# A new hand-written order for a sketched-attention and feed-forward kernel, with other queues for its first loads and all rows of x through DRAM

## The chip, the cores and the metric

The kernel runs on one core of a Trainium2 chip. The metric is the time of one execution on the device, in microseconds. The core has a matrix engine (TensorE, PE in the profile; PEld are its weight loads), VectorE (DVE), ScalarE (ACT), GpSimd (POOL), and SyncE (SP), which here only issues DMAs. ACT can issue DMAs as well. Each engine works through its own instructions in order and waits for the others by semaphores; DMAs issued on SP and on ACT are moved by the core's 16 DMA engines.

## What is computed

```
def phi(x):                                        # x: (b, h, s, 32); S1, S2: (8, 32)
    a = einsum('rd,bhsd->bhsr', S1, x)
    b = einsum('rd,bhsd->bhsr', S2, x)
    return einsum('bhsi,bhsj->bhsij', a, b).reshape(..., 64)
q_p, k_p = phi(q), phi(k)                          # 4 batches, 4 heads, 1088 tokens
kv  = einsum('bhsf,bhsd->bhfd', k_p, v)
z   = k_p summed over s
x   = einsum('bhsf,bhfd->bhsd', q_p, kv) / (einsum('bhsf,bhf->bhs', q_p, z) + 1e-6)
x   = x with the heads side by side                # (4, 1088, 128)
xn  = (x - mean) / sqrt(var + 1e-6) * g_ln         # over the 128 columns
out = x + relu(xn @ w_ch1) @ w_ch2                 # 128 -> 512 -> 128
```

S1, S2 and the two weight matrices arrive as float64 and are turned into float32 on the chip, from their bit fields (the `w_` steps: exponent, mantissa, low word). "Words 0" are S1 and S2, "words 1" w_ch1, "words 2" w_ch2.

## The kernel before

The whole program is one list of steps, `PROGRAM` (lines 910 to 1001). A loop at its end calls the functions named there in that order, and each puts its instructions on the engine that the step names (V VectorE, A ScalarE, G GpSimd, S SyncE) or that the function fixes. There is no planner at run time: the list is the order on every engine, and an engine that waits holds up everything behind it in its own part of the list. A capital A, B, C, D, M, N, O or K in other places names one of the eight PSUM banks.

For each batch b the steps are these. `ld` loads k and q with 128 partitions of 34 rows, `ld_v` and `ld_vr` load v; batch 0's v is loaded whole and turned over by TensorE (`v_flip`, `v_cp`). `turn_g`, `turn_h` and `turn_r` (L434, L457, L452) transpose k and q on VectorE in 32 by 32 blocks; `k_feat` (L506) and `q_feat` (L629) multiply by the sketches, `k_tok` and `q_tok` transpose the features back. `k_prod` forms the 64 products per key, `k_val` (L560) sums them against v, `k_vcp`, `k_spr` and `k_rcp` spread the result for the numerators. `k_sum`, `k_zs`, `k_sc` (L531, L539, L545) and `k_sccp` (L553) bring the denominator into q's weights `skq`, on which `q_feat` depends. `q_ac`, `q_den`, `q_rec`, `q_a2`, `q_prod` and `q_turn` (L677) make the normalised query products, and `num` (L735) multiplies them with kv: 32 matmuls of 32 by 32 tiles at 16 positions of the array, four banks for the four row groups. Batch 0 does the first part of this in its own way (`q_dir`, `q_prod0`, `q_flip`, `fold` for w_ch1 times g, `num0`). Three small masks, `c_m2`, `c_m32` and `c_m8`, are made on VectorE (two instructions each, L206 and L207).

The result comes out transposed (`num_cp`, `num_r`), in chunks c: two per batch of 512 tokens (0 to 7) and two of 128 for what is left over (8 and 9). Per chunk, `hid` (L843) makes one of four blocks j of the hidden layer, `relu` (L851, L853) empties it to `hT`, and `sec` (L859) makes one of four blocks t of the second product. `hT` has two buffers, used in turn in the order of chunks 0, 1, 2, 3, 8, 4, 5, 6, 7, 9. For the statistics and the residual the chunk is needed with tokens on the partitions. Chunks 1 to 7 take it through DRAM: `row_turn` (L797) transposes blocks, `row_wr` (L802) writes, four `row_rd` (L808) read back. Chunks 0, 8 and 9 take it by TensorE: `row_pe` (L787) and a copy, `row_cp`. `st_bn`, `st_ag` and `st_pow` (L816 to L829) give the scale, `fin` (L872) or `fin_a` with `fin_g` (L878, L888) the sum, `store` the output.

`fill` and `bump` (L250, L244) are matmuls on ones whose result nobody reads; they stand where TensorE would wait.

The lines that the change and the prediction touch, beside `PROGRAM`:

## Time and profile before

| | us |
|---|---|
| median of 3 runs | 102.90 (102.72 to 105.06) |
| the profiled execution, whole time | 102.81 |
| its span in the profile | 100.9 |
| TensorE busy in the span | 95.3 |
| VectorE busy | 74.0 |
| GpSimd busy | 58.4 |
| ScalarE busy | 41.3 |
| end of the last `sec` on TensorE, from the span's start | 97.40 |

The profile shows one execution. Times in the views count from the start of the span; the whole time is the span and what lies around it. A busy PE is not the same as a PE at its peak, since matmuls are pipelined. A line that begins with an engine and a line of the kernel (L859) is a group of instructions; "out<-in" are the tiles written and read, a releaser after "<-" is what ended an engine's wait.

DMA before: 81 issues on SyncE and 27 on ScalarE. The page moves 13.85 MB; the transfers between `xd` and x or `xh` are the rows through DRAM.

### The profile page before, as it was taken

The numbers are of one execution on the slowest core, as the hardware profiler recorded it, in microseconds if no ns is written. First come the engines' busy times: TensorE is split into PE (matmuls) and PEld (weight loads), VectorE is DVE, ScalarE is ACT, GpSimd is POOL, SyncE is SP. The second block draws the span as 40 slices with busy tenths as digits, with TensorE's granted clock in tenths as the row PEclk, the third lists the DMA queues.
The fourth block names the chain that finished last, engine by engine and source line by source line (L and its number), as shares of the span: only waits on it lengthen the run. The fifth ranks groups of instructions, "written<-read, shape, count | busy, mean of one in ns | idle before, by whom it ended". The sixth has DMA issues, their size and how long they took to land.

```text
span 100.9 us, 3433 instructions
## 1 busy us (share of the span) xinstructions
PE 95.3 (94%) x1355; PEld 68.7 (68%) x1355; DVE 74.0 (73%) x239; ACT 41.3 (41%) x119; POOL 58.4 (58%) x83
## 2 busy tenths in 40 slices
PE   5988999999999999999999999999999999999960
PEld 5765668656656779656588669854469758959950
DVE  2878989789999599699089549999559079661630
ACT  2863754979700720755513353029640030253000
POOL 7115998999588926912999189809920540057000
PEclk9999999999999999999999999999999999999999
DMA  2989999893008760030023220346146445054242
GB/s 76 272 293 389 353 370 275 272 218 88 3 6 301 212 164 3 6 130 0 6 107 106 47 59 0 109 153 187 55 107 204 143 122 148 1 115 132 77 119 64
DMA packets 12367, 13.85 MB, mean 137 GB/s; under 512 B 2880, under 2 KB 8768, under 8 KB 12352
## 3 DMA queue, kind: packets, MB, share of 16 engines
q1 hardware_dynamic: 9968, 11.67, 38.8%
q10 hardware_dynamic: 2384, 1.97, 6.7%
q8 instruction: 10, 0.16, 0.7%
q14 instruction: 5, 0.04, 0.2%
HBM read 9.57 MB, written 4.06 MB: 135 GB/s over the span
## 4 chain that ended last, share of the span: by engine, by line
PE 78%; DMA 5%; POOL 5%; DVE 2%; ACT 2%; SPq 2%; issue 1%; ACTq 0%; POOLq 0%
PE bankO L859 8%; PE bankM L859 8%; DMA w_raw<-in_moe_w_ch_dram 5%; PE bankN L843 5%; PE bankK L560 5%; PE bankC L843 4%; PE bankK L843 4%; PE bankK L859 4%; PE bankB L843 3%; PE bankA L843 3%; PE bankD L843 3%; PE bankM L250 3%; PE bankA L859 3%; PE bankN L859 3%; POOL ob L888 2%; PE bankA L735 2%
## 5 line engine op out<-in xcount | busy, mean ns | idle before, releaser
L82 POOL TENSOR_TENSOR kp<-kf 128x1024 f32<-128x1024 f32 (+4 forms) x9 | 15.9, 1779 | 0.1
L827 POOL TENSOR_SCALAR va<-mv 128x4 f32<-128x4 f32 (+1 forms) x10 | 2.3, 228 | 18.2 <-DVE mv L822 17.7
L82 POOL TENSOR_TENSOR qp<-a,fq 128x1280 f32<-128x1280 f32 (+1 forms) x5 | 11.1, 2219 | 0.2
L859 PEld LDWEIGHTS bankO<-w,hT 128*128 128x128 f32 x80 | 9.7, 192 | 1.9 <-issue 1.9
L829 POOL TENSOR_TENSOR rstd<-va,mhalf 128x4 f32<-128x4 f32 (+1 forms) x10 | 10.3, 1034 | 0.8
L859 PE MATMUL bankO<-w,hT 128*128 128x128 f32 x80 | 10.4, 277 | 0.0
L859 PEld LDWEIGHTS bankM<-w,hT 128*128 128x128 f32 x72 | 9.0, 192 | 1.9 <-issue 1.9
L677 DVE STREAM_TRANSPOSE qpT<-qp 128x1280 f32<-128x1280 f32 (+1 forms) x7 | 9.6, 1365 | 0.0
L250 PE MATMUL bankM<-ones 128*128 128x256 f32 (+1 forms) x28 | 8.3, 440 | 1.2 <-DVE top L180 1.2
L859 PE MATMUL bankM<-w,hT 128*128 128x128 f32 x72 | 9.3, 275 | 0.0
L816 DVE BATCH_NORM_STATS2 st<-x 128x6 f32<-128x128 f32 x32 | 6.7, 272 | 2.5 <-issue 2.5
L250 PEld LDWEIGHTS bankM<-ones 128*128 128x128 f32 x28 | 5.7, 241 | 2.5 <-DVE top L180 1.2
L851 ACT ACTIVATE hT<-bankC 128x512 f32<-128x512 f32 (+1 forms) x6 | 3.3, 551 | 8.3 <-PE bankB L859 4.7
L843 PE MATMUL bankC<-xT,w 128*128 128x512 f32 x12 | 6.1, 592 | 0.0
L843 PE MATMUL bankN<-xT,w 128*128 128x512 f32 (+1 forms) x14 | 6.1, 516 | 0.0
L851 ACT ACTIVATE hT<-bankN 128x256 f32<-128x256 f32 (+1 forms) x6 | 3.0, 498 | 7.2 <-PE bankN L843 7.2
L82 POOL TENSOR_TENSOR a<-fq,rden 128x160 f32<-128x160 f32 (+1 forms) x6 | 2.8, 463 | 5.2 <-DVE rden L659 4.8
L560 PEld LDWEIGHTS bankK<-kp,vn 128*32 128x32 f32 x288 | 4.2, 110 | 2.3 <-issue 1.1
L851 ACT ACTIVATE hT<-bankK 128x512 f32<-128x512 f32 (+1 forms) x6 | 3.1, 522 | 6.2 <-PE bankK L843 5.3
L457 DVE STREAM_TRANSPOSE qT<-qn 128x512 f32<-128x512 f32 x8 | 5.5, 687 | 0.0
L843 PE MATMUL bankK<-xT,w 128*128 128x512 f32 (+1 forms) x12 | 5.4, 530 | 0.0
L735 PE MATMUL bankD<-qpT,kvr 32*32 32x288 f32 (+1 forms) x64 | 5.2, 386 | 0.0
(235 smaller groups left out, 255.2 us busy)
## 6 DMA issues: line engine op xcount, KB each, us to landing
kn<-in_k_dram SPq DMA_DIRECT2D x3, 544.0 KB, 6.2
qn<-in_q_dram SPq DMA_DIRECT2D x3, 544.0 KB, 6.4
vn<-in_v_dram SPq DMA_DIRECT2D x12, 128.0 KB, 4.5
xd<-xh SPq DMA_DIRECT2D x5, 256.0 KB, 2.6
x<-xd SPq DMA_DIRECT2D x20, 64.0 KB, 2.0
out_dram<-ob SPq DMA_DIRECT2D x19, 64.0 KB, 1.7
out_dram<-ob ACTq DMA_DIRECT2D x13, 64.0 KB, 1.9
w_raw<-in_moe_w_ch_dram SPq DMA_DIRECT2D x2, 256.0 KB, 4.0
```

Of the source, the lines that this page charges most:

```text
L82: by[eng].tensor_tensor(out=o, in0=a, in1=b, op=ALU.mult)
L250: pe.matmul(M[0][:, 0:w], ones[:, 0:P], ones[:, 0:w], start=True, stop=True)
L457: dve.transpose(_ap(dst[b % 2], 0, P, P * 4 * half, [[32, 4], [P, 4], [1, 32]]), src[b][:, 512 * half : 512 * half + 512],)
L560: pe.matmul(KV[D * h : D * h + D, 0:F], vn[b][:, TW * h + D * u : TW * h + D * (u + 1)], kp[:, H * F * u + F * h : H * F * u + F * (h + 1) ...
L677: dve.transpose(_ap(qpT, 0, P, 32 * u0, [[32, u1 - u0], [TW, 8], [1, 32]]), qp[:, H * F * u0 : H * F * u1])
L735: pe.matmul(X[r][D * h : D * h + D, o : o + w], kvr[b % 2][rows, DM * f + D * h : DM * f + D * h + D], qpT[rows, c : c + w], start=(f == 0 ...
L816: dve.bn_stats(out=sts[slot(c)][:, 6 * t : 6 * t + 6], in_=row_ap(c, t))
L827: pool.tensor_scalar(out=vas[slot(c)][:, 0:n], in0=_ap(mvs[slot(c)], 0, P, 1, [[2, n]]), scalar1=1e-6, scalar2=None, op0=ALU.add)
L829: pool.tensor_tensor(out=rstds[slot(c)][:, 0:n], in0=vas[slot(c)][:, 0:n], in1=mhalf[:, 0:n], op=ALU.pow)
L843: pe.matmul(banks[z][:, 0:n], w1[:, P * j : P * (j + 1)], cols(c)[:, a : a + n], start=True, stop=True)
L851: act.activation(o, i, AF.Relu)
L859: pe.matmul(banks[z][:, DM * t : DM * (t + 1)], h[:, 512 * j + P * t : 512 * j + P * (t + 1)], w2[:, DM * j : DM * (j + 1)], start=(j == 0 ...
```

## The change

Three things change in the code. The loop in `num` has its two inner loops exchanged: the four matmuls that follow each other now have four row groups, not four column groups. The set `through_dram` holds all ten chunks. And `PROGRAM` is a new list: nearly every step stands elsewhere, several have another engine or bank. Of its 585 steps, `row_pe` and `row_cp` of chunks 0, 8 and 9 and `sk_0` are gone; for those chunks `row_turn`, `row_wr` and four `row_rd` each come in. The fills are the same in number and length.

Cut to what the text speaks of:

```diff
         for f in range(2):
-            for r in range(4):
-                for h in range(H):
+            for h in range(H):
+                for r in range(4):
                     rows, o = slice(32 * r, 32 * r + 32), 32 * u0
...
-    through_dram = set((1, 2, 3, 4, 5, 6, 7, ))
+    through_dram = set((0, 1, 2, 3, 4, 5, 6, 7, 8, 9))
...
-    ld_w S 1 2 4; c_ones; ld_g A; c_small; c_ac 0; ld_s A 0; ld_s S 1; c_vpad 0; c_kvb; c_vpad 1;
-    fill 1 128; ld S k 0 0 16; c_act; c_pads 1; c_pads 0; fill 4 256; c_iota; ld S k 0 16 34;
-    c_ac 1; c_m2; c_ident; ld_w S 1 0 2; c_m32; c_m8; ld S k 1 0 34; ld S q 0 16 34;
-    w_low A 1 256 512; w_ex V 0 0 32; w_bits V 0 0 32; w_bits V 1 256 512; w_exf A 0 0 32;
-    ld_h S q 0 0; w_mant V 1 256 512; w_mant A 0 0 32; w_ex V 1 256 512; ld S v 0 0 32;
...
+    c_vpad 3; c_ident; ld S k 0 16 34; c_ones; c_kvb; fill 1 128; fill 4 256; c_small; c_iota;
+    c_vpad 1; c_pads 0; c_rest; c_ac 0; ld_s A 0; ld_s A 1; c_act; w_ex V 0 0 32; w_bits V 0 0 32;
+    w_mant A 0 0 32; w_exf V 0 0 32; w_e2 V 0 0 32; w_e3 V 0 0 32; w_addlow V 0 0 32;
+    turn_g k 0 2 4; s_heads G; ld_h A q 0 0; sk; ld S k 0 0 16; c_m2; turn_r k 0; c_m32;
+    turn_g k 0 0 2; sk_8 A; ld_w S 1 0 2; fill 1 128; fill 1 128; w_bits V 1 0 256; w_ex V 1 0 256;
+    sk_d; c_m8; ld S q 0 16 34; ld S v 0 0 32; ld S k 1 0 34; k_feat 0 0 9; k_tok 0 1 0 9;
+    k_tok 0 0 0 9; turn_r q 0; k_prod V 0 6 9; w_low A 1 0 256; w_mant A 1 0 256; sk_b; fill 1 128;
+    w_exf A 1 0 256; sk_2 A; sk_q; w_e2 A 1 0 256; ld_g A; bump 24; k_sum 0; k_zs 0; v_flip 2 D;
+    k_sc 0; v_flip 3 N; fill 1 256; turn_h q 0 1; k_sccp F 0; w_e3 V 1 0 256; turn_h q 0 0;
...
-    w_add G 2 0 512; k_sum 2; num_cp A 0 1 4 8; num_cp A 0 0 4 8; num_cp V 0 3 4 8; hid N 0 3 2 4;
...
+    num_r A 0; w_e2 A 2 0 512; k_sum 2; turn_g k 3 0 4; q_ac V 1 0 4; q_ac V 1 4 9; q_den 1 4 9;
...
+    q_ac V 3 0 4; q_ac V 3 4 9; q_den 3 4 9; q_rec 3 4 9; q_den 3 0 4; sec N 2 1; sec M 3 3;
...
+    num_r A 2; num_cp A 2 3 0 4; num_cp V 2 1 0 4; row_turn 4; st_pow 1; q_prod G 3 0 4; sec M 3 2;
...
+    store A 7 2 0 4; st_pow 9; fin O 9 0; store_r A 9 1; fill 1 256; fill 1 256; store_r S 9 0;
```

The order on the queues that the prediction follows, read off the two lists:

- SyncE's first loads before: half 2 of w_ch1, S2, k of batch 0 in two parts, half 1 of w_ch1, k of batch 1, q of batch 0 in two parts, v of batch 0. After: k of batch 0 in two parts, half 1 of w_ch1, a part of q of batch 0, v of batch 0, k of batch 1, half 2 of w_ch1. ScalarE's before: g, S1. After: S1, S2, the other part of q of batch 0, g, then q of batch 1 and k of batch 2.
- VectorE's first work before: the three masks, words 0 mixed with words 1, then k's transposes. After: words 0, k's transposes with the masks between, then words 1.
- TensorE ahead of the first `hid` before: `k_sum 1`, `num0 0 2`, `k_sc 1`, `num0 2 4`, `k_spr 0`, `q_feat 1`. After: `k_spr 0` and others, `k_sum 1`, `num0 2 4`, `k_sc 1`, `num0 0 2`, `q_feat 1`.
- TensorE between `num 2` and `num 3` after: `k_spr 3`, two `sec`, four short `hid` of chunk 8 and three long of chunk 4 among them, a third `sec`, two more long `hid`.
- GpSimd ahead of `num 3` after: `q_prod G 3 4 9`, `q_a2 G 3 0 4`, `st_pow 1`, `q_prod G 3 0 4`.
- ScalarE's issues: 51 after, with 18 `row_rd`, against 27 with 8; SyncE's 72 after, with 22 `row_rd`, against 81 with 20.

## The prediction

> **What bounds the kernel now.** I read the page's busy shares first, then the busy time by stretch, then the chain that ended last.

> ```profile
> span 100.9 us, 3433 instructions
> PE 95.3 (94%) x1355; PEld 68.7 (68%) x1355; DVE 74.0 (73%) x239; ACT 41.3 (41%) x119; POOL 58.4 (58%) x83
> ```
> ```profile
> 3.72:20.28 16.56, 15.75 (x333) 10.88 (x334) 14.74 (x47) 10.29 (x35) 11.46 (x19) 1.00 0.98 320
> 21.85:97.40 75.55, 75.39 (x981) 55.07 (x980) 56.08 (x178) 28.28 (x80) 43.13 (x47) 1.00 0.34 97
> ```
> ```profile
> 21.16 0.36 PE bankA L629
> ...
> 21.85 0.63 PE bankK L843 x2
> 22.48 0.43 PE bankN L843 x2
> ...
> 23.78 0.44 PE bankO L787 x4
> ...
> 44.11 0.11 PE bankD L787
> ...
> 96.47 0.91 PE bankA L859 x8
> 97.40 0.35 DVE ob L872
> ```

> The second fence gives, for a stretch, its length and then the busy time of PE, PEld, DVE, ACT and POOL, the granted clock, the share of the DMA engines and GB/s. The chain lists start, length and work. Together they cut the run in three. From the first `hid` at 21.85 to 97.40, where the last `sec` is done, PE is busy 75.39 of 75.55 us at full clock: this stretch can shrink only by PE work taken out, and grow by any wait put in. The tail, from 97.40 to the span's end at 100.9, is 3.5 us: one `fin`, then stores. In the start, PE's busy time proves nothing, because `fill` and `bump` pad it; there VectorE is busy 14.74 of 16.56 us and the DMA engines 0.98 of the time. So: start by VectorE and loads, middle by TensorE, a fixed tail.

> The profiled execution took 102.81 us, 1.91 us around its span; the median shown is 102.90. I sum against 102.81. Two per cent of it, about what a measurement of this kernel can tell from no change, puts the lines at 100.75 and 104.87.

> **The start: words and keys first.** What PE has done by the first `hid` is the same list in both orders, so only its date moves. It hangs on VectorE reaching `k_sccp V 1` (L553), which gives `q_feat 1` its last weights.

> ```profile
> 2.07 0.28 DVE L206 TENSOR_SCALAR bit<-row 128x2 int32<-128x2 int32 x1 [0.92 <-POOL row L188]
> ...
> 3.17 0.16 DVE L207 TENSOR_TENSOR m<-bit,head 128x4 f32<-128x4 int32 x1
> 3.72 0.17 DVE L277 TENSOR_SCALAR ex<-s_raw 16x32 uint32<-16x32 uint32 x1 [0.38 <-DMA s_raw<-in_S_dram]
> ...
> 4.20 0.29 DVE L299 TENSOR_SCALAR mant<-bits 128x256 f32<-128x256 uint32 x1
> ...
> 6.40 0.39 DVE L318 SCALAR_TENSOR_TENSOR bits<-w_raw,ex 128x256 uint32<-128x256 uint32 x1
> ...
> 7.83 0.29 DVE L277 TENSOR_SCALAR ex<-w_raw 128x256 uint32<-128x256 uint32 x1 [0.90 <-DMA w_raw<-in_moe_w_ch_dram]
> 8.04 0.42 DVE L323 TENSOR_TENSOR mant<-mant,low 128x256 f32<-128x256 f32 x1
> ...
> 12.76 0.35 DVE L639 STREAM_TRANSPOSE fq<-bankA 128x160 f32<-128x160 f32 x1 [0.16 <-PE bankD L629]
> 13.03 0.19 DVE L382 TENSOR_TENSOR sk<-bankK,m 128x64 f32<-128x64 f32 x1
> ...
> 14.60 0.75 DVE L318 SCALAR_TENSOR_TENSOR bits<-w_raw,ex 128x256 uint32<-128x256 uint32 x1
> ...
> 16.97 0.36 DVE L277 TENSOR_SCALAR ex<-w_raw 128x512 uint32<-128x512 uint32 x1
> ...
> 19.55 0.19 DVE L539 TENSOR_TENSOR zT<-bankK,m 128x32 f32<-128x32 f32 x1 [0.52 <-ACT w L77]
> ...
> 20.28 0.15 DVE L553 TENSOR_REDUCE skq<-bankK 128x8 f32<-128x32 f32 x1
> 21.51 0.20 DVE L452 STREAM_TRANSPOSE kT<-kn 128x64 f32<-128x64 f32 x1
> ...
> 26.72 0.69 DVE L318 SCALAR_TENSOR_TENSOR bits<-w_raw,ex 128x512 uint32<-128x512 uint32 x1
> ...
> 39.75 1.45 DVE L82 TENSOR_TENSOR kp<-kf 128x1280 f32<-128x1280 f32 x1
> ```

> Both orders begin at about 3.72, when the sketch words land. Step by step, up to `k_sccp V 1`:
> - Idle that goes: 0.90 (the first half of w_ch1, now third on SyncE's queue and not fifth), 0.16 and 0.52: 1.58 us.
> - Work that leaves or moves behind: `w_add 1` 0.42 (to POOL), `w_mant 1` 0.29 (to ACT), `sk_0` 0.19 (dropped; nothing reads its result), `w_ex 2` 0.36: 1.26 us.
> - Work that comes in: `k_prod V 0 6 9` is 768 of the 1280 columns that took 1.45, so 0.87; the six mask instructions from 2.07 to 3.33, which lay ahead of the words for nothing, now stand behind them, 1.2; `turn_r k 2` 0.20; `w_exf V` as small as the row at 3.72, 0.17: 2.44 us.
> - The same `w_e3` took 0.39 at 6.40 and 0.75 at 14.60. Between 0 and 0.36 saved I take 0.3, since a third, at 26.72, took 0.69 for twice the columns: the 0.75 is the odd one.
> - A new wait: `v_flip 2` stands ahead of `k_sc 0` in PE's order, so all of VectorE's second half waits for v. By the shapes, k, the half of w_ch1, half of q and v ahead of it are 1.6 MB on SyncE's queue, with 0.26 MB on ACT's: at the 320 GB/s of the first stretch 5.8 us, which from a start between 2.5 and 4 lands v at 8.3 to 9.8, while `k_sc 0` is otherwise due near 9.3. Bounds 0 and 1.0, I take 0.3.

> Sum: -1.58 - 1.26 + 2.44 - 0.3 + 0.3 = -0.4. Then PE: before, `q_feat 1` starts at 21.16, 0.88 after `k_sccp V 1`, because `num0 2 4` and `k_spr 0` still stand between; now only `num0 0 2` does, and it is done before. About 0.1 remains: another -0.75. The first `hid` comes 1.15 earlier, at 20.7; bounds 0 (the loads decide) and -1.7 (no wait for v, all of the 0.36).

> The words' issues on ACT change little of this: before, one half of them already came over ACT's queue. The fills are as many as before; two of them now stand after the last `sec`, beside the tail, at no cost.

> **Rows of x through DRAM.** `row_pe` goes for chunks 0, 8 and 9: 0.44 by the row at 23.78, and 0.11 each for the short ones by the row at 44.11, 0.66 us of PE. In its place come three `row_turn` on VectorE (busy 56.08 of 75.55, so covered), 3 writes and 12 reads (DMA share 0.34 in that stretch, covered), while ACT loses two copies. -0.66; if VectorE's cover were gone they would cost their own length, about 0.7 for the long one.

> **The loop order in `num`.**

> ```profile
> 35.84 0.35 PE bankA L629
> ...
> 36.54 0.37 PE bankK L575 x2
> ...
> 40.63 0.38 PE bankA L735 x4
> ...
> 42.16 1.09 PE bankO L859 x8
> ```

> `q_feat` walks the row groups innermost, as `num` will: its 16 matmuls of 288 columns take 36.54 - 35.84 = 0.70. `num 1` has 32 such and takes 42.16 - 40.63 = 1.53, 0.13 more than twice that. Three full `num` and a shorter one: -0.45 if all of it is order. `num` also accumulates and `q_feat` doesn't, so 0 is the other end; I take -0.4, as the row groups' order is what the two then share.

> **The order of the rest.** After `num 0` the old order had `k_sum 2` and a `hid` of chunk 0 before the first `hid` of chunk 1; the new one has `k_sum 2` alone.

> ```profile
> 27.46 0.31 PE bankK L531 x18
> ...
> 27.68 0.28 ACT L77 COPY xT<-bankC 128x128 f32<-128x128 f32 x1
> ```

> The last copy of chunk 1's columns ends at 27.96, 0.50 after `num 0`; `k_sum 2` covers 0.31: a new wait of +0.2 (bounds 0 and 0.5), and everything on PE stands behind it.

> The first `hid` after tiled matmuls took 0.63, the next 0.43, so a change from tiled to full costs 0.2. The old order has 7 blocks of tiled matmuls after 21.85, the new one 8 (`k_sum 3` and `q_feat 2` stand apart from `k_feat 3`): +0.2. [...]

> What is late next, near the end: `num 3` needs both `q_turn`, and `q_prod G 3 0 4` now stands on POOL behind `st_pow 1`, which waits for VectorE's `st_ag 1`, behind the copies after `num 2`.

> ```profile
> 47.91 1.96 POOL L82 TENSOR_TENSOR qp<-a,fq 128x1024 f32<-128x1024 f32 x1
> ...
> 57.83 1.03 POOL L829 TENSOR_TENSOR rstd<-va,mhalf 128x4 f32<-128x4 f32 x1
> ...
> 64.16 1.47 DVE L677 STREAM_TRANSPOSE qpT<-qp 128x1280 f32<-128x1280 f32 x1
> ```

> From the end of `num 2`: copies and `k_rcp V 3` about 1.2, `st_ag` and the first half of `st_pow` about 0.5, then 1.03, 1.96, 1.47 and four fifths of that, 1.2: 7.4 us. PE has `k_spr 3`, three `sec` near 0.9, four short and five long `hid` (0.22 and 0.86, by the half one's 0.43): 8.2 us. Covered by 0.8; each us beyond that would be a us of PE.

> **Sum.** -1.15 - 0.66 - 0.4 + 0.2 + 0.2 = -1.81, with an unchanged tail: span 99.1, time 101.0; I forecast 100.9, since the fills and small waits that the old order still has between blocks can only partly be repeated. With every term at its good end (-1.7, -0.66, -0.45, 0, 0) it is 100.0, at its bad end (0, -0.66, 0, +0.5, +0.2) 102.85.

> **Rivals.**

> *The loads bound the start.* The DMA engines are at 0.98 there, and what moves to ACT's queue moves no byte less. Then the first `hid` stays at 21.85 and the time is 102.0. Against it: the three VectorE waits that go are mostly not for loads. [...]

> *The gaps go too.* The small waits in the old middle stretch (a `sec` or `hid` held a few tenths by a copy) don't come back and the start is at its good end: 100.0 less some 0.3, 99.7. For it: no engine but PE is over 75% in the middle. Against: nothing in the trace shows how large they are.

> *ACT's queue stalls it (slower).* ACT issues 27 DMAs now and 51 after, of them 18 reads of x and not 8. A read waits for its write, in order, and the relus behind it wait too.

> ```profile
> 52.24 0.37 ACT L77 COPY kvr<-bankK 128x256 f32<-128x256 f32 x1 [2.06 <-DMA xd<-xh]
> ...
> 53.78 0.60 ACT L851 ACTIVATE hT<-bankB 128x512 f32<-128x512 f32 x1 [1.17 <-DMA xd<-xh]
> ...
> 80.45 0.60 ACT L851 ACTIVATE hT<-bankN 128x512 f32<-128x512 f32 x1 [5.40 <-PE bankN L843]
> 80.45 0.32 ACTq L893 DMA_DIRECT2D out_dram<-ob  x1
> ```

> The issue itself is cheap (at 80.45 it runs beside a relu); the wait is not: 2.06 and 1.17. Four times the new order puts the first read after a write on ACT (chunks 0, 1, 5, 7). If PE then had no other work and the 1.17 were left each time, +4.7: 105.6. It crosses 104.87 from 1.0 each. Against it: the two waits shown cost PE nothing, as sec and hid of another chunk stood between, and they do in the new order.

> **Chances.** Forecast 0.45, its own range 99.9 to 101.9, half of it under 100.75; gaps 0.24; loads 0.14; ACT 0.17. Faster by over 2%: 0.22 + 0.24 = 0.46. Within 2%: 0.23 + 0.14 = 0.37. Slower: 0.17. The range that holds 8 in 10 leaves the ACT case out and a little of the gaps case: 99.0 to 103.2.

> **What would show it.** The first `hid` near 20.7 and `k_sccp V 1` near 19.9; if that is 21 or later, with idle for v or w_raw, the loads rival holds. No L787 at all; `num 1` near 1.40 from its first matmul to the next work; PE idle of a few tenths before chunk 1's first `hid`; the last `sec` ending near 95.6. If PE idles by ACT's or POOL's doing in the middle, above 1 us in all, I was wrong there: DMA releasers on ACT point to the slow rival, `qpT` ahead of `num 3` to the POOL chain.

## The result and the profile after

The changed kernel takes 111.64 us in the median of 6 runs (105.63 to 112.29); beside it the kernel before took 102.89 (102.53 to 105.06). Its executions fall into two groups, near 105.6 and near 112; the ratio of 1.028 (95% interval 1.0245 to 1.0317) compares only the shorter group with the shorter executions of before. It is slower either way, and the forecast of 100.9, with its range of 99.0 to 103.2, was wrong. The profiled execution is one of the longer group: 111.98 us, with a span of 110.2. A second profiled execution of the same kernel, 106.40 us with a span of 104.6, belongs to the shorter one; both are used below.

The head of the page of the first:

```profile
span 110.2 us, 3436 instructions
...
PE 104.3 (95%) x1349; PEld 72.9 (66%) x1349; DVE 75.6 (69%) x240; ACT 40.6 (37%) x120; POOL 57.8 (52%) x80
```

The busy time by stretch, cut as in the prediction (length, then PE, PEld, DVE, ACT, POOL, the granted clock, the DMA engines' share, GB/s), first of the longer and then of the shorter execution:

```profile
4.12:28.40 24.28, 23.99 (x330) 15.04 (x331) 16.22 (x52) 11.06 (x35) 11.08 (x18) 1.00 0.64 200
29.58:106.66 77.08, 75.34 (x985) 54.60 (x976) 57.56 (x181) 27.40 (x82) 43.49 (x43) 1.00 0.40 113
```
```profile
3.93:21.43 17.50, 16.90 (x331) 10.97 (x331) 15.74 (x53) 10.76 (x35) 10.74 (x17) 1.00 0.88 281
23.65:101.06 77.41, 75.34 (x984) 54.66 (x976) 57.37 (x180) 27.30 (x81) 42.93 (x43) 1.00 0.40 113
```

The first line of each runs from the sketch words to `k_sccp V 1`, the second from the first `hid` to the end of the last `sec`. Before, these were 16.56 and 75.55 us (by the chain; by the timeline, from which the lines here are cut, the middle ran from 21.78 to 97.36, 75.58). PE is busy as long in the middle as before (75.34, then 75.39), but the stretch is 1.5 and 1.8 longer: PE waits there now. The chain of waits shows the end of the longer execution:

```profile
105.77 0.89 PE bankO L859 x8
106.66 0.87 PE bankM L250 x4
```

From 106.66 to 110.2 are 3.54 us: the tail is what it was. So the whole difference of the spans, 110.2 - 100.9 = 9.3, is 7.8 in the start (first `hid` at 29.58 and not 21.78, by the timeline below) and 1.5 in the middle. In the shorter execution it is 1.9 and 1.8, together 3.7.

The timeline of TensorE tells what happened in the start (start, length, work; several `v_flip` and fills are left out), first the longer and then the shorter execution:

```profile
5.67 0.60 PE L374 MATMUL bankK<-ident,s_f 16*128 16x16 f32 x2 [0.29 <-POOL s_f L82]
...
7.35 0.69 PE L506 MATMUL bankA<-kT,sk 64*32 64x288 f32 x1
...
18.13 2.02 PE L595 MATMUL bankN<-skd,qT 128*128 128x96 f32 x8
...
23.88 0.43 PE L506 MATMUL bankA<-kT,sk 64*32 64x288 f32 x1
...
29.58 0.70 PE L843 MATMUL bankO<-xT,w 128*128 128x256 f32 x2
```
```profile
5.49 0.39 PE L374 MATMUL bankK<-ident,s_f 16*128 16x16 f32 x2
...
7.01 0.40 PE L506 MATMUL bankA<-kT,sk 64*32 64x288 f32 x1 [0.49 <-DVE kT L434]
...
13.49 1.13 PE L595 MATMUL bankN<-skd,qT 128*128 128x96 f32 x8
...
23.65 0.70 PE L843 MATMUL bankO<-xT,w 128*128 128x256 f32 x2
```

The same instructions take 0.69 and 0.40, 2.02 and 1.13. At 23.88 the longer execution does `k_feat 1` in 0.43: from there it runs as fast as the other. Until then TensorE ran at half rate: its fills of 128 columns start 0.21 apart (6.58, 6.79, 7.00), where those of the kernel before start 0.11 apart (4.99, 5.10, 5.21, 5.32). The clock column reads 1.00 all the while, because the trace's record of clock changes has no entry ahead of the first change; that first entry, to full rate, stands at 23.42 us in the longer execution, at 5.24 in the shorter and at 4.79 in the kernel before. So each of the three starts at half rate, and they differ in when it is lifted. In the kernel before, fills of 256 columns start 0.43 apart from 1.76 to 4.74 and 0.21 apart from 9.51 on; the six from 2.61 on take 2.77 us in the longer and in the shorter execution alike. Between the two groups of times are 112.0 - 105.6 = 6.4 us.

PE's longest waits, in the longer execution:

```profile
PE bankM L843 <- ACT ob L878: 1.3, 1, 1.3
PE bankM L250 <- DVE top L180: 1.2, 1, 1.2
PE bankO L843 <- ACT xT L77: 0.4, 1, 0.4
PE bankK L374 <- POOL s_f L82: 0.3, 1, 0.3
```

The first and the third lie in the middle; before, PE waited for nothing there that the view names.

### The profile page after: what moved, and what is told of

Read it like the earlier page. It is cut to its first block, busy times and chain, and to the rows that moved or that the text cites. A ratio compares the mean times of both kernels' runs of the same rounds, so it can differ in the third digit from the quotient of the medians.

```text
span 110.2 us, 3436 instructions
## 1 busy us (share of the span) xinstructions
PE 104.3 (95%) x1349; PEld 72.9 (66%) x1349; DVE 75.6 (69%) x240; ACT 40.6 (37%) x120; POOL 57.8 (52%) x80
## 4 chain that ended last, share of the span: by engine, by line
PE 76%; DMA 13%; POOL 3%; DVE 3%; ACT 2%; issue 1%; ACTq 1%; POOLq 0%; DVEq 0%
DMA qn<-in_q_dram 6%; PE bankK L859 6%; PE bankM L250 6%; PE bankD L843 5%; PE bankK L560 5%; PE bankO L859 4%; PE bankN L859 4%; PE bankC L843 4%; PE bankO L843 4%; PE bankA L843 3%; PE bankM L859 3%; PE bankM L843 3%; DMA xd<-xh 3%; DMA s_raw<-in_S_dram 2%; PE bankN L843 2%; POOL rstd L829 2%
## 5 line engine op out<-in xcount | busy, mean ns | idle before, releaser
L82 POOL TENSOR_TENSOR kp<-kf 128x1024 f32<-128x1024 f32 (+4 forms) x8 | 13.9, 1751 | 2.0 <-PE bankK L560 1.9
L82 POOL TENSOR_TENSOR qp<-a,fq 128x1280 f32<-128x1280 f32 (+1 forms) x6 | 13.5, 2248 | 0.6 <-DVE a L82 0.3
L250 PE MATMUL bankM<-ones 128*128 128x256 f32 (+1 forms) x28 | 11.2, 552 | 1.2 <-DVE top L180 1.2
L829 POOL TENSOR_TENSOR rstd<-va,mhalf 128x4 f32<-128x4 f32 (+1 forms) x10 | 10.8, 1076 | 0.8
L859 PEld LDWEIGHTS bankO<-w,hT 128*128 128x128 f32 x72 | 8.7, 192 | 1.9 <-issue 1.6
L677 DVE STREAM_TRANSPOSE qpT<-qp 128x1280 f32<-128x1280 f32 (+1 forms) x7 | 9.5, 1371 | 0.4 <-POOL qp L82 0.4
L859 PE MATMUL bankO<-w,hT 128*128 128x128 f32 x72 | 9.4, 278 | 0.0
L323 POOL TENSOR_TENSOR mant<-mant,low 128x256 f32<-128x256 f32 (+1 forms) x3 | 2.7, 907 | 11.3 <-ACT mant L296 11.3
L859 PE MATMUL bankM<-w,hT 128*128 128x128 f32 x64 | 7.9, 277 | 0.0
L859 PEld LDWEIGHTS bankM<-w,hT 128*128 128x128 f32 x64 | 7.5, 192 | 0.5 <-issue 0.5
L859 PEld LDWEIGHTS bankK<-w,hT 128*128 128x128 f32 x56 | 6.8, 192 | 1.4 <-issue 0.7
L859 PE MATMUL bankK<-w,hT 128*128 128x128 f32 x56 | 7.2, 277 | 0.0
L843 PE MATMUL bankA<-xT,w 128*128 128x512 f32 x12 | 6.2, 599 | 0.0
L843 PE MATMUL bankD<-xT,w 128*128 128x512 f32 x12 | 6.1, 593 | 0.0
L888 POOL TENSOR_TENSOR ob<-ob,x 128x512 f32<-128x512 f32 x4 | 5.1, 1269 | 1.8 <-ACT ob L878 1.8
L735 PE MATMUL bankD<-qpT,kvr 32*32 32x288 f32 (+1 forms) x64 | 5.9, 386 | 0.0
L735 PE MATMUL bankC<-qpT,kvr 32*32 32x288 f32 (+1 forms) x64 | 5.9, 386 | 0.0
L735 PE MATMUL bankB<-qpT,kvr 32*32 32x288 f32 (+1 forms) x64 | 5.8, 386 | 0.0
L735 PE MATMUL bankA<-qpT,kvr 32*32 32x288 f32 (+1 forms) x64 | 5.8, 384 | 0.0
```

Source lines behind the costliest of these rows:

```text
L82: by[eng].tensor_tensor(out=o, in0=a, in1=b, op=ALU.mult)
L250: pe.matmul(M[0][:, 0:w], ones[:, 0:P], ones[:, 0:w], start=True, stop=True)
L323: by[eng].tensor_tensor(out=t["mant"], in0=t["mant"], in1=t["low"], op=ALU.add)
L677: dve.transpose(_ap(qpT, 0, P, 32 * u0, [[32, u1 - u0], [TW, 8], [1, 32]]), qp[:, H * F * u0 : H * F * u1])
L735: pe.matmul(X[r][D * h : D * h + D, o : o + w], kvr[b % 2][rows, DM * f + D * h : DM * f + D * h + D], qpT[rows, c : c + w], start=(f == 0 ...
L829: pool.tensor_tensor(out=rstds[slot(c)][:, 0:n], in0=vas[slot(c)][:, 0:n], in1=mhalf[:, 0:n], op=ALU.pow)
```

## The experiments

In each diff steps of `PROGRAM` are shown; "..." stands for what is left out. "The kernel before" beside a run was measured along with it on the same chip. The first three runs set two theories against each other. By the throttle theory (later the clock theory) the clock that TensorE is granted makes the two groups of times, and the new head of its list makes full rate come late; by the queue theory late loads and ACT's DMAs make the change slower.

**The changed kernel again**, no edit.

> The changed kernel, unchanged. [...] The queue theory (ACT's DMAs and q of batch 3 hold the middle up, the start is only late by loads) expects the same start in both groups and the difference in the middle stretch.

Six runs: 105.08 to 112.25, median 110.31; before 103.27. Of the 12 runs of this kernel in all, 8 are over 109 and 4 from 105.1 to 106.4, so the shorter execution is the rarer one. Not all of the 8 are late in the same way: 111.33 and 109.31 have a mean granted clock of 0.938 and 0.952, where the profiled long one has 1.00. Those two were released and fell back to half rate, by an estimate from these means and their spans for 14 and 10 us (2 x 0.062 x 109.6, 2 x 0.048 x 107.5); no trace of them is kept.

**The head of TensorE's list, exchanged between the kernels.** First the old head in the changed kernel, then the new head in the old one; none of the steps moved is ever read.

```diff
+    ... fill 1 128; fill 1 128; bump 12; sk; bump 24; ...
-    ... sk; ... fill 1 128; fill 1 128; ... bump 24; k_sum 0; ... bump 12; q_tok 0 1 4 9; ...
```

> The changed kernel with the head of TensorE's list as before: two fills and bump 12 ahead of sk, bump 24 behind it, taken from later places, nothing else moved. Throttle theory: most runs in the lower group or below it, 102 to 104, L506 at 0.43 us, first hid at 21 to 22. Queue theory: no change but what a later k_sum costs, 105.6 and 112 as without it.

```diff
-    ... fill 1 128; fill 1 128; bump 12; ... sk; bump 24; ... sk_b; ... k_val 0; ...
+    ... sk; fill 1 128; fill 1 128; ... sk_b; bump 24; ... k_val 0; bump 12; ...
```

> The kernel before with the head of the changed kernel's TensorE list: two fills moved behind sk, both bumps moved behind k_feat. Throttle theory: slower, with runs up to 6 us above 102.9 and a second group, L506 near 0.69 us in a slow run. Queue theory: 102.9, within 0.5.

The old kernel with the new head takes 106.41 to 107.16 us, 1.040 of before (1.0356 to 1.0447): 4% for the place of matmuls on ones. Its busy time by stretch has the clock's steps in it:

```profile
4.49:7.90 3.41, 1.54 (x9) 0.92 (x7) 2.14 (x9) 1.98 (x7) 0.44 (x1) 1.00 0.96 308
7.90:11.32 3.42, 2.75 (x20) 1.22 (x20) 2.83 (x10) 0.00 (x0) 1.57 (x8) 0.50 1.05 381
11.32:14.73 3.41, 3.41 (x72) 2.39 (x72) 0.51 (x1) 1.93 (x7) 3.27 (x5) 0.50 1.07 386
14.73:18.15 3.42, 3.42 (x80) 2.54 (x80) 3.04 (x11) 1.36 (x4) 1.01 (x2) 1.00 1.06 313
```

The stretches are 3.41 us long because that is the grid on which the clock changes in this trace: full at 4.49, half at 7.90 after a stretch with PE busy 1.54, full again at 14.73 after one that was filled. Its first `hid` comes at 26.11, 4.3 later than before, and the middle keeps its 75.6. Not all of the 4.3 is the clock's, since in this execution a load was late too:

```profile
7.25 0.71 DVE L434 STREAM_TRANSPOSE kT<-kn 128x512 f32<-128x512 f32 x1 [1.18 <-DMA kn<-in_k_dram]
```

VectorE waited 1.18 us for the second part of k, and `k_feat 0` began at 8.57 and not 7.08. Another version of the old kernel, at the end of this section, had `k_feat 0` at 8.81 with the clock held from 7.18 on, and its first `hid` at 23.47; so, by an estimate, 26.11 - 23.47 = 2.6 or more is the half rate's. It was there in all four executions: their mean granted clocks are 0.961 to 0.968.

The changed kernel with the old head takes 105.13 to 110.46, median 108.27. It is no clean trial. TensorE was at full rate at 5.69 and the start ran well until 19, but then:

```profile
21.35 0.37 ACT L77 COPY w<-bankD 128x256 f32<-128x256 f32 x1 [3.07 <-DMA kn<-in_k_dram]
```
```profile
21.77 0.33 PE L690 MATMUL bankD<-ident,kvd 128*128 128x128 f32 x1 [2.60 <-ACT w L77]
```

ACT stood 3.07 us with the issue of `ld_v A 1 0` at its head, and PE behind it 2.60, after which the clock fell to half for 6.83 us. The DMAs of both kernels share eight semaphores, and in the traces of before and after none of the 51 and 63 issues that can be compared goes out ahead of the landing of the DMA that had its semaphore. In the kernel before, three on SyncE go out at 7.83, 9.19 and 15.46 and follow landings at 7.81, 9.18 and 15.45. With the fills moved, the compiler handed the semaphores out in another order: the one for `ld_v A 1 0` had been k of batch 3's, and the issue went out at 20.96, as that landed; in the changed kernel itself it had been g's. In the experiments on the changed kernel below it is g's again.

**The loop order in `num`**, alone in the old kernel.

```diff
-            for r in range(4):
-                for h in range(H):
+            for h in range(H):
+                for r in range(4):
```

> The kernel before with the two inner loops of num exchanged, nothing else. The order theory of the prediction: 0.4 us faster, num 1 at 1.40 us. Rival (the order of row and column groups makes no difference, since all 16 tile positions are in flight at once): 0.0, num 1 at 1.53 us.

102.95 us, ratio 1.0037 (0.9996 to 1.0079). In the chain of waits `num 1` stands, with the new order, between these lines:

```profile
40.74 0.35 PE bankA L735
...
42.26 0.02 PE bankD L735
42.27 0.75 PE bankO L859 x5
```

42.27 - 40.74 = 1.53, to the hundredth what it was. In the changed kernel `num 2` and `num 3` take 1.53 as well.

**The clock held in the changed kernel's head.** Full-width matmuls without a gap from 1.17 to `k_feat 0`.

```diff
-    ... sk; ... fill 1 128; fill 1 128; ... k_feat 0 0 9; ... ld_g A; bump 24; k_sum 0; ...
+    ... fill 1 128; fill 1 128; sk; bump 24; ... fill 1 256; k_feat 0 0 9; ... ld_g A; k_sum 0; ...
```

> [...] Rival, the late words or the loads set the start: moving matmuls that nobody reads changes nothing, the median stays above 109 and the first hid near 29.6.

105.94 to 108.84 in four runs, median 107.14: the release came early (4.86), but the median is above the 107 that I expected with an early release. The stretches on the grid show full rate lost again:

```profile
4.86:8.28 3.42, 3.42 (x78) 2.37 (x76) 2.98 (x14) 1.79 (x6) 1.08 (x2) 1.00 0.97 329
8.28:11.69 3.41, 2.85 (x54) 1.43 (x66) 3.19 (x8) 2.50 (x10) 2.54 (x8) 1.00 1.02 331
11.69:15.10 3.41, 3.41 (x51) 1.70 (x33) 2.60 (x6) 0.46 (x2) 2.70 (x4) 0.50 0.74 246
15.10:18.52 3.42, 3.42 (x12) 2.65 (x12) 1.58 (x8) 1.64 (x5) 0.00 (x0) 0.50 1.00 348
```

It went at 11.69, after a stretch in which PE was busy 2.85 of 3.41, about half of it with 32 by 32 tiles, most of them `v_flip`. And the third stretch here was busy from end to end and lifted nothing: it held `q_feat`, `v_flip` and 1.0 us of full-width work. In the changed kernel itself four such stretches stand between 6.36 and 20.01, all of them busy 3.41 or 3.42 us and none of them enough; the one up to 23.42, with fills, `bump` and `k_val`, was. So TensorE's busy time alone doesn't tell which stretch lifts the half rate. Nor does the 128 by 128 work alone: the four stretches held 1.8, 0.7, 1.4 and 2.5 us of it, and the one that lifted the half rate 1.9, beside 1.6 of `bump` and `k_val` on 128 by 32.

**`v_flip` side by side.**

```diff
-    ... k_zs 0; v_flip 2 D; k_sc 0; v_flip 3 N; ... v_flip 1 O; q_feat 0 4 9; fill 1 128; v_flip 0 M; ...
+    ... v_flip 2 D; v_flip 3 N; v_flip 1 O; v_flip 0 K; fill 1 128; ... q_feat 0 4 9; ...
```

> Packing theory: with the four v_flip side by side their 32 matmuls hold TensorE 0.67 us at full rate or 1.3 at half (after: 1.73 and 3.28), and the first hid comes about 1.0 us earlier than in a run of after at the same rate. Rival, VectorE bounds the start: the v_flip shrink as much, but the first hid comes less than 0.3 us earlier, because TensorE then waits for VectorE.

Inconclusive: the four held PE 0.84 us, but PE then waited 2.0 us for their copies (`q_feat 0` writes bank D), lost full rate from 15.48 to 18.89, and the first `hid` came at 25.36; 107.43 in one run. The copies were late because the edit put them behind two loads in ACT's list, whose issue waited for earlier DMAs: ACT stood 3.08 us ahead of the first copy, until a load of w_ch1 had landed. So the same question was put to the old kernel, where the rest stands still:

```diff
-    ... q_dir 0 4 O; ... v_flip 1 K; ... v_flip 2 N; ... v_flip 0 D; ... v_flip 3 C; ... k_feat 1 0 9; ...
+    ... v_flip 1 K; q_dir 0 4 O; v_flip 2 N; ... fill 1 128; v_flip 0 D; k_feat 1 0 9; v_flip 3 C; ...
```

> Before with the four v_flip put apart again (q_dir, one moved fill and k_feat 1 between them), banks and number of matmuls unchanged. Packing theory: their 32 matmuls hold TensorE 1.7 us in place of 0.67, and because the start's TensorE queue is in order and full, the first hid and the time move by +0.6 to +1.0. Rival, fills only pad the start and VectorE bounds it: v_flip cost the same 1.7, but the first hid stays within 0.2 of 21.85 and the time within 0.3 of before.

105.06 to 105.51, ratio 1.018 (1.0125 to 1.0243). The timeline of TensorE (in its last gap stands `k_feat 1`):

```profile
12.94 0.79 PE L466 MATMUL bankK<-v,ident 32*32 32x256 f32 x8
13.66 1.13 PE L595 MATMUL bankO<-skd,qT 128*128 128x96 f32 x8
14.72 0.63 PE L466 MATMUL bankN<-v,ident 32*32 32x256 f32 x8
15.28 0.49 PE L250 MATMUL bankM<-ones 128*128 128x128 f32 x2
15.70 0.63 PE L466 MATMUL bankD<-v,ident 32*32 32x256 f32 x8
...
16.91 0.63 PE L466 MATMUL bankC<-v,ident 32*32 32x256 f32 x8
```

Before, the same 32 stood side by side:

```profile
13.65 0.42 PE L466 MATMUL bankK<-v,ident 32*32 32x256 f32 x4
...
13.99 0.39 PE L466 MATMUL bankC<-v,ident 32*32 32x256 f32 x4
14.32 0.43 PE L506 MATMUL bankA<-kT,sk 64*32 64x288 f32 x1
```

Each `v_flip` of eight matmuls takes about 0.6 alone. Before, the 32 ran from 13.65 to 14.32 in all, 0.67, each `v_flip` on its own rows of the array. The first `hid` moved by 2.3, to 24.11; 1.7 of that is `v_flip`, counted from each start to the next work; the head of this execution was also later (`k_feat 0` by 0.2, PE's wait for `skd` 0.7 and not 0.4). That is more than the +1.0 expected, and the rival, by which nothing moves, is out: TensorE's list counts in the start.

**`turn_r q 3` later on VectorE.**

```diff
-    k_sccp V 3; turn_r q 3; st_bn 0; st_ag 0; ... turn_h q 3 1; ...
+    k_sccp V 3; st_bn 0; st_ag 0; ... turn_r q 3; turn_h q 3 1; ...
```

> Queue theory: turn_r q 3 stands ahead of st_bn 0 on VectorE and waits for a load that ACT issued late; behind turn_h's neighbours instead, st_bn 0 to fin_a M 0 run about 1.5 us earlier, and TensorE's wait for bank M before hid M 3 0 falls from 1.3 to under 0.3; from the first hid to the end of the last sec 77.0 becomes 75.7. Rival, the rows of chunk 0 come back late themselves or POOL's step holds the chain: the wait stays above 1.0.

The timeline of all engines, first of the changed kernel, then of this one:

```profile
53.45 0.25 DVE L452 STREAM_TRANSPOSE qT<-qn 128x64 f32<-128x64 f32 x1 [1.61 <-DMA qn<-in_q_dram]
53.62 0.83 DVE L816 BATCH_NORM_STATS2 st<-x 128x6 f32<-128x128 f32 x4
...
55.14 2.38 POOL L829 TENSOR_TENSOR rstd<-va,mhalf 128x4 f32<-128x4 f32 x1
...
57.55 0.37 ACT L878 ACTIVATE ob<-bankM,rstd 128x128 f32<-128x128 f32 x1 [1.97 <-POOL rstd L829]
...
58.75 1.12 PE L843 MATMUL bankM<-xT,w 128*128 128x512 f32 x2 [1.35 <-ACT ob L878]
```
```profile
51.75 0.86 DVE L816 BATCH_NORM_STATS2 st<-x 128x6 f32<-128x128 f32 x4
...
53.30 2.38 POOL L829 TENSOR_TENSOR rstd<-va,mhalf 128x4 f32<-128x4 f32 x1
...
55.71 0.37 ACT L878 ACTIVATE ob<-bankM,rstd 128x128 f32<-128x128 f32 x1
...
57.23 1.02 PE L843 MATMUL bankM<-xT,w 128*128 128x512 f32 x2
```

Read from the bottom: PE waits for bank M, which `fin_a M 0` empties, which needs chunk 0's `rstd`, which needs `st_bn 0`, which stood on VectorE behind a transpose whose load had not landed. ACT issued that load at 46.55, after its reads of x. With the transpose moved the whole chain is 1.87 earlier at `st_bn` and PE doesn't wait; the middle takes 104.95 - 29.56 = 75.4 in place of 77.1. The start of this execution was at half rate until 23.46, as in the longer ones; 110.27.

**All three, and `num_cp` of chunk 1 first.**

> All three together and num_cp of chunk 1 ahead of that of chunk 2. If the three causes add up: 105.1 (after's lowest) less 1.0 for v_flip, 1.3 for turn_r q 3 and 0.2 for num_cp gives 102.6, with most runs within 1 us of it, level with before's 102.9. If VectorE takes over as the bound of the start: about 103.6. If the clock theory is wrong: a median above 107.

104.27 to 106.24, median 104.41, ratio 1.011 (1.0044 to 1.0179): above both sums. Its middle is 75.4, so that part holds; the rest is the start: the profiled execution lost full rate at 11.12 for 6.83 us, with PE waiting 1.1 for `v_cp` ahead of `q_feat 0` (its copies, too, stand behind the two loads, and ACT stood 3.13), and the others, at 104.3 to 104.5, are still 1.4 above before.

**The same with `v_flip` where before had them, and the gaps filled.**

```diff
+    ... ld_g A; fill 1 256; k_sum 0; k_zs 0; fill 1 256; k_sc 0; ... q_dir 0 4 N; ... q_tok 0 2 4 9;
+    v_flip 1 K; v_flip 2 O; v_flip 0 D; v_flip 3 C; ... fill 1 256; fill 1 256; bump 12; ...
```

> After with before's head on TensorE and one more fill, a fill in each of the two gaps behind sk_b and ahead of k_sc 0, the four v_flip side by side behind q_dir as in before, turn_r q 3 later, num_cp of chunk 1 first. If clock, packing and turn_r q 3 are the whole difference: first hid near 22.0, from there to the last sec 75.4, tail 3.5, so about 102.8, level with before. If the start of after has a further cost of its own: first hid at 23.0 or later and 104 or more.

103.04 to 104.27 in nine of ten runs and one of 105.94; ratio 1.0043 (1.0000 to 1.0087), median 104.05 beside before's 103.94 on this chip. Nearly all of the changed kernel's loss is recovered. The middle is 75.37, and the first `hid` comes at 22.70: between the two expectations, 0.9 later than before. What is left of the start is VectorE's:

```profile
4.21 0.17 DVE L277 TENSOR_SCALAR ex<-s_raw 16x32 uint32<-16x32 uint32 x1 [3.06 <-DMA s_raw<-in_S_dram]
...
8.37 0.48 DVE L516 STREAM_TRANSPOSE kf<-bankB 128x288 f32<-128x288 f32 x1 [0.45 <-PE bankB L506]
...
17.76 0.61 DVE L318 SCALAR_TENSOR_TENSOR bits<-w_raw,ex 128x256 uint32<-128x256 uint32 x1 [0.51 <-ACT ex L311]
...
20.84 0.19 DVE L539 TENSOR_TENSOR zT<-bankK,m 128x32 f32<-128x32 f32 x1 [0.61 <-ACT w L77]
...
21.70 0.15 DVE L553 TENSOR_REDUCE skq<-bankK 128x8 f32<-128x32 f32 x1
```

From 4.21 to `k_sccp V 1` at 21.70 VectorE is busy 15.60 us, where the old order had 14.74, and idle as long as there (1.89 and 1.82): three new waits, 0.45 + 0.51 + 0.61 = 1.57, stand where the old order had 0.90 + 0.16 + 0.52 = 1.58.

**Nothing but fills**, in the changed kernel, to separate the clock from the rest. The fill ahead of `q_dir` overwrites bank M before `v_cp` has read head 0 of v from it, so the values of that head are lost; the work is the same.

```diff
+    ... fill 1 128; fill 1 128; sk; bump 24; ... fill 1 256; k_feat 0 0 9; ... fill 1 256; k_sum 0;
+    k_zs 0; ... fill 1 256; k_sc 0; ... fill 1 256; q_dir 0 4 N; ...
```

> After with nothing changed but unread full-width matmuls: two fills ahead of sk, bump 24 behind it, one more fill of 256 each ahead of k_feat 0, k_sum 0, k_sc 0 and q_dir. If the granted clock is the cause of the long times: released before 8 us, not lost in the start, times from 105 to 106.5 and none over 108, though TensorE has about 1.5 us more unread work. If the long times come from elsewhere: still over 109 in most executions.

105.45 to 107.11 in four runs, one of them above the 106.5 expected, none near 111. Released at 4.50 and never lost, with the middle (77.4) and the `v_flip` left as they were. The long times of the change are the clock's.

**Chunk 0 through DRAM**, alone in the old kernel.

```diff
-    through_dram = set((1, 2, 3, 4, 5, 6, 7, ))
+    through_dram = set((0, 1, 2, 3, 4, 5, 6, 7, ))
...
-    ... row_pe 0 O; q_turn 4 9; ... row_cp A 0 O; ... num 0 4 9; ... st_bn 0; ... turn_g k 3 0 4; ...
+    ... q_turn 4 9; row_turn 0; row_wr S 0; ... num 0 4 9; row_rd S 0 3; row_rd S 0 1; row_rd S 0 2;
+    row_rd S 0 0; ... turn_g k 3 0 4; st_bn 0; ...
```

> Before with chunk 0's rows of x through DRAM (row_pe 0 and row_cp 0 gone, one row_turn, one row_wr and four row_rd more, st_bn 0 a little later on VectorE). The prediction's term: TensorE holds 0.53 us less between the first hid and the last sec, so 75.0 in place of 75.6 and 102.3 us. Rival: row_turn's 0.67 on VectorE and the transfers push a later step, the saving is below 0.2.

103.53 us (10 runs), ratio 1.0031 (0.9975 to 1.0087). `row_pe`'s 0.53 is gone, and PE spends it again: from each start to the next, `num` takes 0.29 more, `hid` 0.29 and `k_feat` 0.25, as `row_turn` puts VectorE's copies and transposes 0.6 later. The middle is 75.85, 0.3 longer than before.

**The old kernel with more unread work**: with chunk 0 through DRAM and two additions (first), with one addition alone (second), with both (third).

```diff
-    ... sk; bump 24; ... k_feat 0 0 9; ... sk_b; ...
+    ... sk; bump 40; ... k_feat 0 0 9; ... fill 1 128; sk_b; ...
```

> The kernel with chunk 0 through DRAM, and full-width work added where TensorE waits in the first 9 us (bump 24 becomes bump 40 ahead of k_feat 0, one more fill ahead of sk_b). Clock theory: fewer executions release the clock late, so the times lie closer together, 102.2 to 103.0 with none over 104 in most rounds. Rival: the added work delays the start by its own 0.4 us and the spread stays (one in three near 104.4).

> Before with bump 24 ahead of k_feat 0 made bump 40, in a gap of 0.3 us. If a late release is what gives the kernel before its times over 104: at most one in six over 104, the median near 102.9. If not: one in three or more over 104 as in before on the same chip.

> As b_hold1, and a fill of 128 more ahead of sk_b. If the clock is the cause: none over 104, the median 102.9 to 103.4, below before's on the same chip when that has long times in a third of its executions. If not: as before, and 0.2 us longer.

The first: 103.44 to 104.04 in 12 runs, beside 29 runs of before from 102.69 to 107.00, of which 14 are over 104.3. They lie closer together, as expected, but above the 102.2 to 103.0 expected, and 0.5% above the shorter executions of before (ratio 1.0050, 1.0018 to 1.0081). The second, only `bump 40`: 102.76 to 103.73 in 12 runs, median 103.03, beside 23 runs of before from 102.56 to 105.64, median 103.43, of which 8 are over 104. The third: 103.20 to 104.47, median 103.92, with four of 12 over 104 where none was expected.

That the kernel before pays for a late release in its executions over 104, and that the longer `bump` takes this away, is not shown: none of its long executions was profiled. There is a rival, seen in the profiled execution of the third, 104.47, in which full rate came at 7.18:

```profile
7.50 0.71 DVE L434 STREAM_TRANSPOSE kT<-kn 128x512 f32<-128x512 f32 x1 [1.67 <-DMA kn<-in_k_dram]
```
```profile
8.81 0.40 PE L506 MATMUL bankA<-kT,sk 64*32 64x288 f32 x1 [0.74 <-DVE kT L452]
```

The second part of k was late. VectorE waited 1.67 us for it, `k_feat 0` began at 8.81 and the first `hid` at 23.47; in the profile of the second these are 0.23, 7.73 and 21.95. The first `hid` is 1.5 later, and so is the end: 104.47 us and 103.01. So a late load makes an execution of the old order long too, and how the long ones divide between load and clock stays open. The shorter executions with `bump 40` don't become shorter (ratio 1.0000, 0.9971 to 1.0028), so it wins by its median and its worst time only; it is the best version found.

## Why the prediction was wrong

- **The step that failed first** is the start's ground: "What PE has done by the first `hid` is the same list in both orders, so only its date moves", with "The fills are as many as before ... at no cost". The list is the same, its speed isn't. The change moved fills and bumps from ahead of and behind `sk` to later places, and left 0.29 idle ahead of `sk` and tiles behind; full rate then came at 23.42 and not near 5, or, in two long executions without a trace, came and was lost again (mean granted clocks of 0.938 and 0.952). Shown from both sides: the new head costs the old kernel 4%, more fills alone take the changed kernel from a median of 110 or more to 106.2. The term was taken as 0; it is up to about 6.4 (112.0 - 105.6), in two thirds of the executions.
- **`v_flip` was not a term.** I priced one more block of tiles at 0.2 and did not see that four `v_flip` side by side run at once and apart do not: +1.1 in the shorter execution (1.73 against 0.67, from each start to the next work), +1.7 in the old kernel.
- **"Idle that goes: 1.58" went and came back** as 1.57 of new waits, for PE, for `ex` and for a copy of ACT. An engine that waits less here is early for the next one. The words landed no earlier: the first work on them begins between 3.78 and 4.21 in the profiled executions with the new loads, between 3.72 and 4.11 in those with the old. The work in and out of the list was near right: +2.44 - 1.26 - 0.3 is 0.9 more for VectorE, and its busy time up to `k_sccp V 1` rose from 14.74 to 15.74 in the shorter execution and to 15.60 with the steps mended. With the idle time back, `k_sccp V 1` came at 21.43 and 21.70, not near 19.9.
- **`w_e3`, -0.3, had the wrong sign.** The moved one took 0.94 and 1.35 in the two executions of the changed kernel, against 0.75 in the old place, and 0.51 in the run with nothing but fills; the two rows I had of 256 columns, 0.39 and 0.75, were no bounds. The wait for v, +0.3, did not come; VectorE waited instead 0.47 for q of batch 0 and 0.28 for k of batch 2 in the shorter execution, and for no load that the view names in the version with the steps mended.
- **The loop order: 0, not -0.4.** I had a bound at 0 and took the other end, from `q_feat`, which differs in more than the order.
- **Rows through DRAM:** no L787 is left, as forecast, and PE saves 0.75 in the profile (0.66 forecast), but the trial in the old kernel shows that it needn't reach the end: what `row_turn` pushes back on VectorE is work that PE waits for. I had it covered, since VectorE is busy 56.08 of 75.55.
- **The middle:** the wait of 0.4 ahead of chunk 1's first `hid` lay in its bounds (0 to 0.5). The chain I named as late next, on POOL ahead of `num 3`, did not strike. The wait for bank M, 1.3 to 1.7, I had not seen as such; it has the form of the third rival, a DMA issued late on ACT and an engine waiting in order behind it, though on VectorE, once, and not after a read of x. That rival's 105.6 beside the shorter executions' 105.6 is chance: the reads after writes that it priced cost PE nothing that the view names.
- **The tail** was right: 3.5.

That the executions in which the clock is early still need 105.1 to 106.4 comes for the most part from these smaller steps: with `v_flip`, `turn_r q 3` and the copies of chunk 1 mended, and the clock held, nine of ten executions of the same order take 103.0 to 104.3. What each of the three is worth there was not taken apart.

One thing stays open. In two of the shorter starts PE shows a wait of 0.5 and 0.8 inside `q_feat 1` that the view puts down to "issue"; no run tells what it is, and it makes up part of the 23.65.

## What to carry to other kernels

Matmuls that nobody reads can be worth more than their time: moved to later places they made the old kernel 4% slower, and more of them took the changed kernel from a median of 110 or more to 106.2. Before moving one, compare the length of one and the same matmul early and late in the trace (here 0.69 and 0.43), since the clock column is silent until the first change. Small matmuls on different tiles of the array belong side by side: the four `v_flip` took 0.67 together and 1.73 apart, as a list with other work between them pays each block in full. And a wait taken out of one engine's list is worth only what the next wait of that engine leaves of it (1.58 went here, 1.57 came): follow it one step on before adding it up.
